# Routing temporaries in PSUM, one reduce for the maxima of k, and a new prologue order

## The chip, the core and the metric

The kernel runs on one core of a Trainium2 chip. Its engines work side by side, each through its own queue in order: PE (TensorE, matrix products and transposes), DVE (VectorE) and ACT (ScalarE) for elementwise work and reductions, POOL (GpSimd) for elementwise work and indirect transfers, SP, whose queue starts most DMAs. SBUF and PSUM are the memories that they read and write; PE writes PSUM alone. The metric is the device time of one execution in microseconds.

## The reference

Three stages follow each other; `k` is normalised over the sequence, `q` over the head.

```python
def _attn_ref(q, k, v):                       # (4, 8, 576, 64)
    q_s = np.exp(q - np.max(q, axis=-1, keepdims=True))
    q_s = q_s / (np.sum(q_s, axis=-1, keepdims=True) + 1e-09)
    k_s = np.exp(k - np.max(k, axis=2, keepdims=True))
    k_s = k_s / (np.sum(k_s, axis=2, keepdims=True) + 1e-09)
    kv = np.einsum('bhsd,bhse->bhde', k_s, v)
    return np.einsum('bhsd,bhde->bhse', q_s, kv)
...
    # _moe_ref: x is (2304, 512), 8 experts 512 -> 1024 -> 512
    noisy_logits = x @ w_gate + np.log1p(np.exp(x @ w_noise)) * noise
    top2 = np.argpartition(-noisy_logits, 2, axis=1)[:, :2]
    ...                                       # softmax over the two
        h = np.maximum(x[mask] @ w1[e], 0.0)
        out[mask] += top2_w[mask, k, None] * (h @ w2[e])
...
    # _moe2_ref: 512 -> 2048 -> 512
    g = P / (Q + 1e-06)                       # P cubic, Q quadratic in h = x @ w_in
    return g @ w_out
```

## The kernel before

Tokens lie on the 128 partitions. The 2304 tokens are 18 tiles of 128: batch `b` gives four tiles of its first 512 tokens (partition p holds tokens 4p to 4p+3, the index `r`), and tiles 8 and 17 hold the last 64 tokens of two batches each (the remainders `kr`, `qr`, `vr` with index `j`). Tiles 0 to 8 are the first half, 9 to 17 the second.

Matrix products in fp32 accuracy for the experts and the last stage take three matmuls (`mm3`, lines 726 to 728): operands are split in a high part, made by ACT, and a low part, made by DVE or POOL. Before that part, called the main loop here, lies a prologue, whose order on every engine is written out by hand: the string `ORDER` names steps (`kmx.1` is step `kmx` with argument 1) and each step issues its instructions in that place, under `tc.manual_schedule`; `REST` follows among the first transposes of the main loop, and `LOADS` orders the loads on SP. A generator step (`rt`, `rl`, `rw`) runs on to its next `yield`. An engine does its instructions in that order and waits for what each needs.

The steps of the prologue:

- k of batch b: `kmx` the maximum over r (DVE, three tensor_tensors over 512 elements), `kmT` transposes it (PE), `kmm` reduces over the partitions' tokens and takes the larger of that and the remainder's `mr` (`krT`, `krm`), `kmB` spreads the maximum (PE, tile `pm`), `ksb` subtracts (DVE, tile `ek`), `kex` (ACT) the exponential, `ksm` (POOL) sums over r, `kz` (PE) over partitions.
- `kv` (PE) is the product of k and v, tile `pk`; `kvn` normalises it into `KV` (name `kvx`, DVE); `kvT`, `kvc` transpose it, `kg` multiplies it with the gate weights and `kgc` copies these 64 columns behind it in `KV`, so that one product with q gives the output of attention and the logits.
- q of batch b: `qmx`, `qsb` (POOL), `qex` (ACT), `qsm` (sum, plus epsilon, reciprocal), `qnm` (POOL, the product). The remainders do the same in `rmx`, `rex`, `rsm`, `rnm`.
- tile T of X: `xT` transposes q (PE), `xc` copies (ACT), `xp` is the product (`px`, two banks of the pool psW), `xo` copies it out (ACT), `xs` stores it as rows of `Xrows` (SP), `xg` sums its logits into `L` (DVE).
- `rt.g`, the routing of half g (`route`): noise, top two of eight, each token's place in its expert's list (`base` is a matmul with counts) and one-hots `oc`, `ocv`, `oh`, three chunks of each, from which `rl` (PE) makes lists; `slots` makes gather and scatter indices; `rw` makes the weights of the two experts. Names in the rows: `u`, `w`, `sp`, `mk`, `ma`, `sc`, `cf`, `ov`.
- expert 0 begins in the prologue on tokens of the first half: `aw` loads its weights, `sa.i` (ACT) and `sv.i` (POOL, line 913; `sv.0.V` on DVE) make high and low parts (`w10l` to `w21l`, two pieces each), `ag` gathers the tokens `xga` (POOL's indirect DMA), `at`, `ac`, `al` (PE, ACT, DVE: `xa`, line 941) transpose and split them; `m1`, `mb` are its first product (`pha`), `mr`, `ml` relu and split, `m2`, `mc` the second (`acca`).

PSUM has eight banks: psT two (`t0`, `t1`), psK two (`k0`, `k1`: `krT`, `kmT`, `pm`, `pk`, `kvT`, `xTa`, `pha` in turn), psW two pairs.

Of the kernel before, what the change touches and what calls it, by code (L numbers as in the profile page):

```python
# [1 line left out]

# [21 lines left out]
E = 8  # L24
# [33 lines left out]
    xg.4 qmx.2 kv.0.2 kv.0.3 qsm.0 rmx.1 qnm.0.1 kz.0 xg.5 rex.1 krm.1 qnm.1.2 kvn.0 kmT.3 qnm.1.3 xT.6 kvT.0
    qmx.3 xc.6 qnm.0.0 xT.7 kvc.0 xp.6 qsb.2 xc.7 xT.1 xo.6 xg.6 xp.7 kmm.3 xc.1 xs.4 xT.0 rsm.1 xo.7 kmB.3 xg.7
    aw.0.0 xc.0 kg.0 ksb.3 qsb.3 qex.2 xT.8 kmT.2 xc.8 aw.0.1 kgc.0 kex.3 kmm.2 xp.1 qnm.0.3 qsm.2 kmB.2 xp.8  # L60
    qnm.0.2 xo.1 xs.5 ksm.3 qex.3 xs.6 xT.2 ksb.2 kv.3.0 aw.1.0 xo.8 xT.3 kv.3.1 xc.2 xc.3 xg.8 sa.0 kv.3.2 xg.1
    qsm.3 xs.8 sa.1 xp.3 aw.1.1 qnm.2.3 kz.3 xo.3 qnm.2.2 kex.2 xg.3 xp.0 sv.0.V kv.3.3 xs.3 xp.2 xs.7 xo.0
    qnm.3.3 xg.0 kvn.3 sa.2 kv.2.0 xs.0 qnm.3.1 xs.1 xg.2 xT.16 rt.0 kv.2.1 ksm.2 xc.16 rt.0 rt.0 xo.2 rt.0
    kv.2.2 sa.3 xs.2 xT.14 kvT.3 xc.14 kv.2.3 kvc.3 kg.3 sa.4 sv.2 kz.2 sa.5 kgc.3 xp.16 kvn.2 sa.6 rt.0 rw.0
    xg.16 xT.12 xo.16 sv.3 rt.0 xp.14 sa.7 xs.16 kvT.2 xo.14 xc.12 xs.14 qnm.3.2 xg.14 xT.11 kvc.2 rt.0 xc.11
    rt.0 xT.15 rw.0 kg.2 xc.15 rt.0 xp.15 qnm.3.0 kgc.2 rt.0 xp.12 xo.15 rt.0 xs.15 xT.13 rt.0 xo.12 rl.0 xc.13
    xs.12 qnm.2.0 xg.15 rl.0 rt.0 xp.13 rt.0 xT.9 xo.13 rt.0 xc.9 xs.13 qnm.2.1 xg.13 rl.0 xg.12 xp.11 rt.0
# [1218 lines left out]
```

## Time and profile before

| what | value |
|---|---|
| median of three runs | 997.84 us (997.36 to 998.83) |
| the profiled execution | 1000.78 us |
| its span, first to last instruction | 998.8 us |
| PE busy | 944.9 us, 95% of the span |
| DVE, ACT, POOL busy | 778.8, 589.4, 283.0 us |
| PE's largest share of the chain that ended last | lines 726 to 728 |
| mean granted clock of PE | .983 of full speed |

The profile cuts the span in 40 slices of 25 us. PE's busy share in tenths reads 2 8 7 7 6 8 9 9 and then 9 in every slice but the last one (8): the first six or seven slices are the prologue. There are two kinds of rows. Timelines give the start in us, the length in us, the engine, the line of the kernel, the operation, what it writes and reads with the shapes, and how many instructions the row joins (x2); in brackets how long the engine was idle before, and whom it waited for. Grouped rows give a sum and the mean of one in ns.

### The profile page before, as it was taken

The numbers are of one execution on the slowest core, as the hardware profiler recorded it, in microseconds if no ns is written. First come the engines' busy times: TensorE is split into PE (matmuls) and PEld (weight loads), VectorE is DVE, ScalarE is ACT, GpSimd is POOL, SyncE is SP. The second block draws the span as 40 slices with busy tenths as digits, with TensorE's granted clock in tenths as the row PEclk, the third lists the DMA queues.
The fourth block names the chain that finished last, engine by engine and source line by source line (L and its number), as shares of the span: only waits on it lengthen the run. The fifth ranks groups of instructions, "written<-read, shape, count | busy, mean of one in ns | idle before, by whom it ended". The sixth has DMA issues, their size and how long they took to land. (4 is left out here: it accounts for less than half of the span.)

```text
span 998.8 us, 15516 instructions
## 1 busy us (share of the span) xinstructions
PE 944.9 (95%) x5296; PEld 845.4 (85%) x5296; DVE 778.8 (78%) x1564; ACT 589.4 (59%) x1188; POOL 283.0 (28%) x279
## 2 busy tenths in 40 slices
PE   2877689999999999999999999999999999999998
PEld 1766678988888888888898999899899999999997
DVE  5887786868677878777871169999989898798785
ACT  3265415545454646455551168787777787787775
POOL 5577422212221212121222133222323222132221
...
GB/s 242 283 214 98 116 14 244 249 161 262 151 243 179 243 205 224 226 200 244 201 173 191 214 320 182 53 95 54 1 74 1 1 43 1 32 1 1 32 1 32
DMA packets 91148, 137.37 MB, mean 138 GB/s; under 512 B 15698, under 2 KB 44374, under 8 KB 91064
## 3 DMA queue, kind: packets, MB, share of 16 engines
...
## 5 line engine op out<-in xcount | busy, mean ns | idle before, releaser
L1141 POOL TENSOR_TENSOR hlr<-vr,hhr 128x384 fp32r<-128x384 f32 x95 | 105.1, 1109 | 287.7 <-ACT hhr L1140 219.4
L726 PE MATMUL phr<-xhr,wih 128*128 128x384 f32 x384 | 129.8, 338 | 0.0
L728 PE MATMUL phr<-xhr,wil 128*128 128x384 f32 x384 | 129.3, 337 | 0.0
L727 PE MATMUL phr<-xlr,wih 128*128 128x384 f32 x384 | 129.0, 336 | 0.0
L791 DVE SCALAR_TENSOR_TENSOR hl<-ph,hh 128x256 fp32r<-128x256 f32 (+4 forms) x120 | 56.6, 471 | 77.8 <-ACT hh L790 75.0
L790 ACT ACTIVATE hh<-ph 128x256 fp32r<-128x256 f32 (+4 forms) x120 | 50.5, 421 | 110.5 <-PE ph L728 104.6
L727 PE MATMUL accr<-wol,hhr 128*128 128x512 f32 x288 | 113.4, 394 | 0.0
L726 PE MATMUL accr<-woh,hhr 128*128 128x512 f32 x288 | 112.7, 391 | 0.0
L728 PE MATMUL accr<-woh,hlr 128*128 128x512 f32 x288 | 109.7, 395 | 0.0
L1129 DVE SCALAR_TENSOR_TENSOR sqr<-sqr,coef,abr 128x384 f32<-128x384 f32 x96 | 64.4, 670 | 35.3 <-ACT sqr L1128 35.3
L756 POOL DMA_INDIRECT xg<-Xrows,gidx x35 | 39.2, 1119 | 160.0 <-PE xT L772 158.4
L1124 ACT ACTIVATE vr<-phr,coef 128x384 f32<-128x384 f32 x96 | 64.1, 668 | 33.1 <-PE phr L728 25.2
L1136 DVE SCALAR_TENSOR_TENSOR sqr<-sqr,qone,abr 128x384 f32<-128x384 f32 x96 | 71.9, 749 | 9.3 <-ACT abr L1135 5.2
L718 POOL DMA_INDIRECT Yrows<-y,sidx x35 | 38.8, 1109 | 135.6 <-ACT y L811 127.2
L1134 ACT ACTIVATE abr<-sqr,qone 128x384 f32<-128x384 f32 x96 | 59.7, 623 | 26.5 <-DVE sqr L1129 26.3
L726 PE MATMUL ph<-xh,w11h 128*128 128x256 f32 (+4 forms) x240 | 75.3, 314 | 0.0
L726 PEld LDWEIGHTS phr<-xhr,wih 128*128 128x128 f32 x384 | 72.2, 188 | 3.4
L727 PEld LDWEIGHTS phr<-xlr,wih 128*128 128x128 f32 x384 | 72.1, 188 | 3.3
L726 PE MATMUL ph<-xh,w10h 128*128 128x256 f32 (+4 forms) x240 | 72.3, 302 | 1.0 <-ACTq L1056 1.0
L727 PE MATMUL ph<-xl,w10h 128*128 128x256 f32 (+4 forms) x240 | 72.7, 303 | 0.1
L728 PE MATMUL ph<-xh,w11l 128*128 128x256 f32 (+4 forms) x240 | 72.6, 302 | 0.0
L727 PE MATMUL ph<-xl,w11h 128*128 128x256 f32 (+4 forms) x240 | 72.4, 302 | 0.0
(293 smaller groups left out, 2652.3 us busy)
## 6 DMA issues: line engine op xcount, KB each, us to landing
...
```

Source lines behind the costliest of these rows:

```text
L718: st = G.indirect_dma_start(out=Y, out_offset=bass.IndirectOffsetOnAxis(ap=idx, axis=0), in_=yt, in_offset=None, bounds_check=2 * NTOK - 1 ...
L726: PE.matmul(o, ah, bh, start=first, stop=False)
L727: PE.matmul(o, ah, bl, start=False, stop=False)
L728: return PE.matmul(o, al, bh, start=False, stop=last).ins
L756: G.indirect_dma_start(out=g[0:self.rows(t)], out_offset=None, in_=X, in_offset=bass.IndirectOffsetOnAxis(ap=self.cols(gidxE, gidx, t), ax ...
L790: a_ = A.activation(hh, ph, AF.Relu)
L791: v_ = V.scalar_tensor_tensor(hl, ph, 0.0, hh.bitcast(F32), op0=ALU.max, op1=ALU.subtract)
L1124: A.activation(v, ph, AF.Identity, scale=coef[:, 3:4], bias=coef[:, 2:3])
L1129: V.scalar_tensor_tensor(sq, sq, coef[:, 5:6], ab, op0=ALU.mult, op1=ALU.add)
L1134: A.activation(r0, sq, AF.Ln, bias=qone)
L1136: V.scalar_tensor_tensor(sq, sq, qone, r0, op0=ALU.add, op1=ALU.mult)
L1141: (V if self.end and f == NF2 - 1 else G).tensor_tensor(gl, v, gh.bitcast(F32), op=ALU.subtract)
```

## The change

- PSUM: psK gets three banks, psW one pair (all `px` tiles take turns on it), and a new pool psR one bank, `route{g}`.
- `route` puts its temporaries in that bank in such a way that each DVE instruction of the chain has an operand there: `u`, `u2`, `sp`, `mk`, `idx`, `po`, `ov2`, `cf`, `ti`, `tr`, later `ma`, `s2`, `oc`, `lvp` in the same columns. `w`, `u3`, `sc`, `ov`, `tj` stay in SBUF; `mk[:, 1]` is copied to SBUF, since both inputs of `ma` would be in PSUM. The counts `rt` come from a reduce. The list values stay in the bank and are copied out once; the weights move from POOL to DVE, with copies of places and experts.
- `kmx` is one tensor_reduce over r, a view with r innermost. The remainder's maxima lie beside those of `kmT`, so that `kmm` is two reduces. `rmx` negates in its reduce.
- epsilon is added by ACT (`qse`, `rse`), `qsm` and `rsm` keep the sum and the reciprocal (`qrc`).
- `kgc` copies by ACT.
- `ORDER` is another one; `LOADS` begins with `kr0`; `mc.6` moves to `REST`.

```diff
-    km1a km1b kr0 qm1 km0 - qr0 - vm1 - vr0 ...
+    kr0 km1a km1b qm1 km0 - qr0 - vm1 - vr0 ...
...
-    xs.9 xg.10 xs.17 rt.1 sv.6 xo.10 rt.1 at.1 at.0 xs.10 ac.1 ac.0 al.1 rt.1 al.0 sv.7 rt.1 m1.0 m1.1 mb.1 sv.4
+    xo.16 xg.16 xc.10 xp.9 rw.0 sv.4 rw.0 rw.0 xo.9 xg.9 xs.9 xp.10 xs.16 sv.5 xg.10 at.1 rt.1 at.0 ac.1 rt.1
+    ac.0 al.1 rt.1 al.0 xo.10 rt.1 m1.0 xs.10 mb.0 m1.1 mr.0 m1.2 mb.1 mb.2 mr.1 mr.2 ml.0 rt.1 rw.1 ml.1 rw.1
...
-    psW = early.enter_context(tc.tile_pool(name="psW", bufs=2, space=PSUM))
-    keyb, qTb = Turn(psK, "k0", "k1"), Turn(psT, "t0", "t1")
+    psW = early.enter_context(tc.tile_pool(name="psW", bufs=1, space=PSUM))
+    keyb, qTb = Turn(psK, "k0", "k1", "k2"), Turn(psT, "t0", "t1")
+    psR = early.enter_context(tc.tile_pool(name="psR", bufs=1, space=PSUM))
...
-        V.tensor_reduce(m, st["kmT", b], axis=AX.X, op=ALU.max)
-        V.tensor_tensor(m, m, st["mr", b // 2][:, :, b % 2], op=ALU.max)
+        mr = st["mr", b // 2][:, b % 2]
+        V.tensor_reduce(mr[:, :, 0], st["kmT", b], axis=AX.X, op=ALU.max)
+        V.tensor_reduce(m, mr, axis=AX.X, op=ALU.max)
...
-    def kgc(b):
-        V.tensor_copy(KV[b][:, :, 2 * HD:], st["pg", b])
+    def kgc(b, eng=A):
+        copy(eng, KV[b][:, :, 2 * HD:], st["pg", b])
...
-        V.tensor_scalar_add(t, t, 1e-9)
-        V.reciprocal(t, t)
+    def plus_eps(t):
+        A.activation(t, t, AF.Identity, bias=eps)
...
-        u = W("u", [P, TP, E], F32, g)[:, 0:n]
-        w = W("w", [P, TP, E], F32, g)[:, 0:n]
-        sp = W("sp", [P, TP, E], F32, g)[:, 0:n]
+        bank = psR.tile([P, 512], F32, tag="r", name=f"route{g}")
+        u, u2, sp = (B_(TP, E) for _ in range(3))
+        mk = B_(2, E, TP)
+        idx, po, ov2, cf = (B_(TP, 2) for _ in range(4))
+        ti, tr = (B_(TP, 2, dt=I32) for _ in range(2))
+        e1s[g] = B_(TP), po, idx
+        at_[0] = 0
+        ma, s2 = (B_(E, TP) for _ in range(2))
+        at_[0] = 0
+        oc = B_(TH * 2, NCOL)
+        lvp = B_(NCOL)
...
-        V.scalar_tensor_tensor(u, w, 1.0, u, op0=ALU.subtract, op1=ALU.subtract)
-        V.scalar_tensor_tensor(u, z, 0.0, u, op0=ALU.max, op1=ALU.subtract)
-        V.tensor_tensor(sp, sp, u, op=ALU.add)
+        V.scalar_tensor_tensor(u2, w, 1.0, u, op0=ALU.subtract, op1=ALU.subtract)
+        V.scalar_tensor_tensor(u3, z, 0.0, u2, op0=ALU.max, op1=ALU.subtract)
+        V.tensor_tensor(sp, sp, u3, op=ALU.add)
...
-        V.tensor_tensor(ma, mk[:, 0], mk[:, 1], op=ALU.add)
+        V.tensor_copy(mk1, mk[:, 1])
+        V.tensor_tensor(ma, mk[:, 0], mk1, op=ALU.add)
...
-        V.tensor_copy(rt, sc[:, :, n - 1])
-        V.tensor_tensor(sc, sc, ma, op=ALU.subtract)
+            V.tensor_reduce(rt, ma, axis=AX.X, op=ALU.add)
+        V.tensor_tensor(s2 if g else sc, sc, ma, op=ALU.subtract)
...
-        V.tensor_scalar(sm, e1, 1.0, 1e-9, op0=ALU.add, op1=ALU.add)
-        V.reciprocal(sm, sm)
-        yield
-        G.tensor_copy(wts[:, ts_, 0], sm)
-        G.tensor_tensor(wts[:, ts_, 1], e1, sm, op=ALU.mult)
+        V.tensor_scalar(e1, e1s[g][0], 1.0, 1e-9, op0=ALU.add, op1=ALU.add)
+        V.reciprocal(wts[:, ts_, 0], e1)
+        V.tensor_tensor(wts[:, ts_, 1], e1s[g][0], wts[:, ts_, 0], op=ALU.mult)
+        V.tensor_copy(pos[:, ts_], e1s[g][1])
+        V.tensor_copy(idf[:, ts_], e1s[g][2])
```

The step `kmx` is in both kernels the same function; `ORDER` of before calls it as `kmx.1.V` (its second branch) and now as `kmx.1` (its first, `km[b].rearrange("p h r d -> p h d r")`).

POOL, around the gather of expert 0's first tokens (`xga`; `eq_...` and `qr_...` are q, `e_0`, `e_1` the weights of the two halves), before:

```order
L404 TENSOR_TENSOR qr_183<-qr_183,qrs_443 128x512
L918 DMA xga_1006<-Xrows,gidxA 128x512
L918 DMA xga_1008<-Xrows,gidxA 128x512
L615 COPY wts<-smw_827 128x9
L616 TENSOR_TENSOR wts<-e_0_826,smw_827 128x9
L913 TENSOR_TENSOR w10l_673<-raw_531,w10h_634 128x1024
L913 TENSOR_TENSOR w21l_1058<-raw_654,w21h_821 128x1024 x2
L913 TENSOR_TENSOR w20l_1136<-raw_615,w20h_800 128x1024 x2
L608 TENSOR_TENSOR e_1_1180<-mv_1085 128x9
```

and now:

```order
L944 TENSOR_TENSOR w10l_691<-raw_523,w10h_669 128x1024
L406 TENSOR_TENSOR eq_518<-eq_518,qs_620 128x512
L406 TENSOR_TENSOR eq_475<-eq_475,qs_609 128x512
L944 TENSOR_TENSOR w11l_809<-raw_601,w11h_708 128x1024
L944 TENSOR_TENSOR w21l_932<-raw_664,w21h_828 128x1024
L406 TENSOR_TENSOR eq_475<-eq_475,qs_609 128x512
L944 TENSOR_TENSOR w21l_932<-raw_664,w21h_828 128x1024
L949 DMA xga_999<-Xrows,gidxA 128x512
L949 DMA xga_1001<-Xrows,gidxA 128x512
L639 TENSOR_TENSOR e_0_1027<-mv_758 128x9
L944 TENSOR_TENSOR w20l_1029<-raw_634,w20h_807 128x1024 x2
L639 TENSOR_TENSOR e_1_1160<-mv_1082 128x9
```

The pieces of `w10l` and `w21l` stood behind the gather and stand ahead of it now; behind it are those of `w20l`.

DVE, at the maxima of batches 2 and 3 (`kmx_382`, `kmx_399` before, `kmx_347`, `kmx_374` now; `kvx` is KV, `mx`, `qs` belong to q), before:

```order
L335 TENSOR_TENSOR kvx_111<-pk_279,rz_332 64x4x64 x2
L293 TENSOR_TENSOR ek_339<-km_144,pm_297 128x8x4x64
L296 TENSOR_TENSOR kr_139<-kr_139,pm_297 64x512
L354 COPY kvx_111<-pg_363 128x4x16
L261 TENSOR_TENSOR kmx_382<-km_164 128x512
L263 TENSOR_TENSOR kmx_382<-kmx_382,km_164 128x512 x2
L261 TENSOR_TENSOR kmx_399<-km_171 128x512
L263 TENSOR_TENSOR kmx_399<-kmx_399,km_171 128x512 x2
L451 TENSOR_REDUCE L<-px_386 128x16
L358 TENSOR_REDUCE mx_417<-qm_174 128x32
L374 TENSOR_REDUCE qs_429<-eq_337 128x32
```

and now:

```order
L340 TENSOR_TENSOR kvx_112<-pk_287,rz_342 64x4x64 x2
L272 TENSOR_REDUCE kmx_347<-km_168 128x512
L272 TENSOR_REDUCE kmx_374<-km_175 128x512
L385 TENSOR_REDUCE qs_390<-eq_325 128x32
L412 RECIPROCAL qrs_327<-qrs_327 128x8
L261 TENSOR_REDUCE mr_425<-krT_354 128x4x2
L402 RECIPROCAL qs_390<-qs_390 128x32
L458 TENSOR_REDUCE L<-px_418 128x16
L369 TENSOR_REDUCE mx_437<-qm_178 128x32
L419 TENSOR_REDUCE mxr_452<-qr_187 128x8
```

The two chains of three instructions are one reduce each, and follow `kvn.1` (`kvx`) directly; `ksb.0` (`ek_339`), which stood between, is earlier now, and the copy from `pg` is gone from this engine.

DVE, at the end of the first half's routing block (`sc`, `rt`), before:

```order
L521 SCALAR_TENSOR_TENSOR sc_764<-seg,ma_762 128x72
L524 CAST rt_766<-sc_764 128x8
L525 TENSOR_TENSOR sc_764<-sc_764,ma_762 128x72
L354 COPY kvx_113<-pg_795 128x4x16
L331 TENSOR_SCALAR rz_816<-pz_804 128x4
L332 RECIPROCAL rz_816<-rz_816 128x4
L335 TENSOR_TENSOR kvx_112<-pk_698,rz_816 64x4x64 x2
L451 TENSOR_REDUCE L<-px_811 128x16
```

now:

```order
L551 SCALAR_TENSOR_TENSOR sc_726<-seg,route_722 128x72
L555 TENSOR_REDUCE rt_783<-route_722 128x8
L556 TENSOR_TENSOR sc_726<-sc_726,route_722 128x72
L336 TENSOR_SCALAR rz_823<-pz_811 128x4
L337 RECIPROCAL rz_823<-rz_823 128x4
L340 TENSOR_TENSOR kvx_113<-pk_682,rz_823 64x4x64 x2
L458 TENSOR_REDUCE L<-px_818 128x16
```

and ACT there now (`w..h` are high parts of expert 0's weights, `qTs` transposed q):

```order
L937 ACTIVATE w11h_708<-raw_601 128x1024
L435 ACTIVATE qTs_792<-qT_746 128x512
L363 ACTIVATE xo_799<-px_700 128x512
L937 ACTIVATE w20h_807<-raw_634 128x1024
L363 ACTIVATE kvx_114<-pg_802 128x4x16
L937 ACTIVATE w20h_807<-raw_634 128x1024
L937 ACTIVATE w21h_828<-raw_664 128x1024
L363 ACTIVATE xo_852<-px_818 128x512
```

The copy from `pg` into `kvx` stood behind the subtraction on DVE and is among the high parts on ACT now.

## Rows read from the trace of the kernel before

**Rows 1.** Stretches (us; busy us per engine, granted clock, DMA share, GB/s).
```profile
127.30:160.00 32.70, 31.21 (x194) 27.65 (x195) 24.43 (x108) 6.63 (x17) 8.54 (x11) 0.92 0.29 97
```

**Rows 2.** Waits of PE, 0 to 160 us (total us, times, longest).
```profile
PE pha L726 <- DVE xa L941: 8.0, 1, 8.0
...
PE px L434 <- DVE kvx L354: 7.4, 2, 5.8
...
PE kmT L275 <- DVE rz L331: 6.2, 1, 6.2
...
PE pm L285 <- DVE m L280: 3.6, 2, 2.5
```

**Rows 3.** Timeline 117 to 128 us (start, length in us; idle before in brackets).
```profile
117.91 8.69 DVE L497 TENSOR_SCALAR w<-u 128x72 f32<-128x72 f32 x1 [0.62 <-ACT u L495]
...
121.90 4.63 POOL L913 TENSOR_TENSOR w20l<-raw,w20h 128x1024 fp32r<-128x1024 f32 x2
...
126.52 1.28 DVE L941 TENSOR_TENSOR xa<-xTa,xa 128x512 fp32r<-128x512 f32 x2
```

**Rows 4.** Timeline, first and second half's routing.
```profile
84.53 0.73 DVE L497 TENSOR_SCALAR w<-u 128x72 f32<-128x72 f32 x1 [0.62 <-ACT u L495]
...
85.29 3.67 DVE L501 SCALAR_TENSOR_TENSOR u<-w,u 128x72 f32<-128x72 f32 x1
...
97.46 1.04 POOL L404 TENSOR_TENSOR qr<-qr,qrs 128x512 f32<-128x512 f32 x1
...
97.51 0.21 DVE L354 COPY kvx<-pg 128x64 f32<-128x64 f32 x1
...
127.72 0.22 DVE L501 SCALAR_TENSOR_TENSOR u<-w,u 128x72 f32<-128x72 f32 x1
...
132.69 0.23 DVE L525 TENSOR_TENSOR sc<-sc,ma 128x72 f32<-128x72 f32 x1
```

**Rows 5.** DVE by line and shape, 0 to 160 us (busy us, mean ns | idle).
```profile
L263 DVE TENSOR_TENSOR kmx<-kmx,km 128x512 f32<-128x512 f32 x8 | 10.3, 1285 | 0.2
...
L358 DVE TENSOR_REDUCE mx<-qm 128x32 f32<-128x2048 f32 x4 | 9.1, 2267 | 0.0
...
L570 DVE TENSOR_TENSOR oh<-rowb,itR 128x768 bf16<-128x768 bf16 x6 | 5.7, 952 | 0.0
...
L567 DVE TENSOR_TENSOR ocv<-oc,vhl 128x288 bf16<-128x288 bf16 x12 | 5.0, 458 | 0.3
...
L261 DVE TENSOR_TENSOR kmx<-km 128x512 f32<-128x512 f32 x4 | 3.8, 957 | 1.4 <-DMA km<-in_k_dram 1.4
...
L540 DVE TENSOR_REDUCE pos<-mk 128x18 f32<-128x144 f32 x2 | 0.8, 421 | 0.1
...
L533 DVE TENSOR_TENSOR sc<-sc,base 128x72 f32<-128x72 f32 x2 | 0.4, 224 | 0.0
```

**Rows 6.** Timeline 99 to 118 us, around the px of the second half.
```profile
99.86 0.21 PE L530 MATMUL base<-rt,tri 128*128 128x8 bf16 x1
...
100.86 1.05 ACT L906 ACTIVATE w21h<-raw 128x1024 fp32r<-128x1024 f32 x1
...
112.35 0.60 ACT L441 ACTIVATE xo<-px 128x512 f32<-128x512 f32 x1 [1.10 <-PE px L434]
...
112.98 0.23 DVE L451 TENSOR_REDUCE L<-px 128x16 f32<-128x64 f32 x1 [0.81 <-ACT xo L441]
...
113.02 4.00 PE L434 MATMUL px<-kvx,qTs 128*128 128x144 f32 x32
```

**Rows 7.** Timeline, k and q part.
```profile
33.60 2.29 DVE L293 TENSOR_TENSOR ek<-km,pm 128x2048 f32<-128x2048 f32 x1
...
55.22 7.20 POOL L366 TENSOR_TENSOR eq<-qm,mx 128x2048 f32<-128x2048 f32 x2
...
59.64 2.80 DVE L280 TENSOR_TENSOR m<-m,mr 128x4 f32<-128x4 f32 x1
```

**Rows 8.** Stretch, columns as in rows 1.
```profile
127.30:129.00 1.70, 1.66 (x6) 1.44 (x7) 1.49 (x6) 0.00 (x0) 0.00 (x0) 0.50 0.00 0
```

More of the change, by code (lines that the diff above doesn't have):

```diff
@@ L1 @@
 from contextlib import ExitStack, contextmanager, nullcontext
+from math import prod
 import concourse.bass as bass
@@ L51 @@
 LOADS = """
-    km1a km1b kr0 qm1 km0 - qr0 - vm1 - vr0 - qm0 - vm0 - km2 - kr1 - km3 - qm2 - vm2 - vr1 qr1 qm3 vm3
+    kr0 km1a km1b qm1 km0 - qr0 - vm1 - vr0 - qm0 - vm0 - km2 - kr1 - km3 - qm2 - vm2 - vr1 qr1 qm3 vm3
 """
 ORDER = """
-    kmx.1.V krT.0 krm.0 kmT.1 kmm.1 qmx.1 kmB.1 ksb.1 qsb.1 rmx.0 kex.1 kmx.0.V qex.1 ksm.1 kmT.0 kv.1.0 kmm.0
-    rex.0 kmB.0 qsm.1 kv.1.1 kv.1.2 rsm.0 qmx.0 kv.1.3 qnm.1.0 kz.1 qnm.1.1 kvn.1 qsb.0 ksb.0 kvT.1 xT.5 kvc.1
-    xT.4 xc.5 xc.4 kg.1 rnm.0 krT.1 kex.0 kgc.1 xp.5 kmx.2.V xp.4 kv.0.0 xo.4 kmx.3.V xo.5 qex.0 kv.0.1 ksm.0
@@ L58 @@
[L58 to L67, printed above, removed]
@@ L73 @@
-    mc.5 m2.7 mc.6
+    krT.0 krm.0 kmx.1 kmT.1 qmx.1 kmm.1 qsb.1 kmx.0 kmB.1 ksb.1 kmT.0 qex.1 kmm.0 kex.1 qsm.1 kmB.0 ksm.1 kv.1.0
+    ksb.0 qse.1 kv.1.1 kv.1.2 qrc.1 kex.0 qmx.0 kv.1.3 qnm.1.2 kz.1 rmx.0 qsb.0 rex.0 kv.0.0 kvn.1 kmx.2 kvT.1
+    krT.1 kv.0.1 rse.0 kvc.1 qnm.1.3 qex.0 xT.6 kmx.3 qnm.1.1 xT.7 kv.0.2 qnm.1.0 xc.6 qsm.0 xc.7 xT.5 ksm.0
+    kg.1 xc.5 xT.4 kgc.1 rsm.0 xp.7 xc.4 krm.1 qse.0 kv.0.3 qrc.0 xo.7 xg.7 qmx.2 xp.4 xo.4 qnm.0.0 kz.0 rmx.1
+    xg.4 rnm.0 rex.1 kvn.0 xp.5 qsb.2 xg.5 kmT.3 kmT.2 qmx.3 kvT.0 rse.1 xT.0 xo.5 xT.8 kvc.0 xp.6 kmm.3 qsb.3
@@ new lines @@
+    xc.0 xg.6 aw.0.0 kmB.3 kmm.2 xo.6 kg.0 xc.8 rsm.1 ksb.3 kmB.2 kgc.0 qex.2 xp.0 qnm.0.3 xs.4 xo.0 xs.6 rnm.1
+    xg.0 xT.3 kex.3 ksb.2 xp.8 xs.7 qnm.0.2 xs.0 qnm.0.1 xs.5 xT.2 qex.3 kv.3.0 aw.0.1 ksm.3 xg.8 qsm.2 kv.3.1
+    xc.2 xo.8 qsm.3 qse.2 xp.2 xc.3 xs.8 kex.2 aw.1.0 xT.1 kv.3.2 qrc.2 xg.2 qnm.2.2 kz.3 qse.3 xo.2 qnm.2.3
+    kv.3.3 qrc.3 aw.1.1 xc.1 qnm.3.0 sa.0 xp.3 kvn.3 qnm.3.1 kv.2.0 xo.3 xg.3 sv.0.V sa.1 kvT.3 xs.3 xp.1 kvc.3
+    xs.2 sa.2 xT.14 qnm.3.2 xg.1 xT.13 rt.0 kv.2.1 ksm.2 xc.14 rt.0 rt.0 xT.15 xc.13 rt.0 kv.2.2 sa.3 xc.15
@@ L139, in fused_kernel, with slots @@
     marks, tiles = {}, {}
-    def slots(pool, lv, n, gi, si, nm):
-        lt = pool.tile([P, n], F32, name=f"lt{nm}")
-        lu = pool.tile([P, n], F32, name=f"lu{nm}")
+    def slots(pool, lv, n, gi, si, nm, tmp=None):
+        lt, lu = tmp or [pool.tile([P, n], F32, name=f"l{x}{nm}") for x in "tu"]
         V.tensor_scalar(lu, lv, float(NTOK), float(-NTOK), op0=ALU.is_gt, op1=ALU.mult)
@@ L351, in kg, with copy, qmx @@
             PE.matmul(pg[:, c], st["kvc", b][:, c, :], wgn[:, c].rearrange("p k e -> p (k e)"), start=True, stop=True)
-    def kgc(b):
-        V.tensor_copy(KV[b][:, :, 2 * HD:], st["pg", b])
-    def qmx(b):
+    def kgc(b, eng=A):
+        copy(eng, KV[b][:, :, 2 * HD:], st["pg", b])
+    def copy(eng, o, i):
+        if eng is A:
+            A.activation(o, i, AF.Copy)
+        else:
+            eng.tensor_copy(o, i)
+    def qmx(b, neg=None):
         mx = st["mx", b] = pw.tile([P, H, R], F32, tag="mx", name=f"mx{b}", bufs=2)
-        V.tensor_reduce(mx, qm[b], axis=AX.X, op=ALU.max)
+        V.tensor_reduce(mx, qm[b], axis=AX.X, op=ALU.max, negate=neg is not None)
     def eq(b):
@@ L490, in route, with B_ @@
         z = L[:, ts_, E:G2E]
-        u = W("u", [P, TP, E], F32, g)[:, 0:n]
-        w = W("w", [P, TP, E], F32, g)[:, 0:n]
-        sp = W("sp", [P, TP, E], F32, g)[:, 0:n]
+        bank = psR.tile([P, 512], F32, tag="r", name=f"route{g}")
+        at_ = [0]
+        def B_(*shape, dt=F32):
+            k = prod(shape)
+            a = bank[:, at_[0]:at_[0] + k]
+            at_[0] += k
+            if dt != F32:
+                a = a.bitcast(dt)
+            ax = "abcd"[:len(shape)]
+            return a.rearrange(f"p ({' '.join(ax)}) -> p {' '.join(ax)}", **dict(zip(ax, shape)))
+        u, u2, sp = (B_(TP, E) for _ in range(3))
[8 more added lines that the diff above has]
+        lvp = B_(NCOL)
+        w = W("w", [P, TP, E], F32, g)
+        u3 = W("u3", [P, TP, E], F32, g)
+        mk1, sc = (W(x, [P, E, TP], F32, g) for x in ("mk1", "sc"))
+        ov = W("ov", [P, TP, 2], F32, g)
+        lt, lu = (W(x, [P, CC], F32, g) for x in ("lt", "lu"))
         A.activation(u, z, AF.Abs)
@@ L981, in fused_kernel @@
     STEPS = {f.__name__: f for f in (krT, krm, kmx, kmT, kmm, kmB, ksb, kex, ksm, kv, kz, kvn, kvT, kvc, kg, kgc,
[L982 removed]
+                                     qmx, qsb, qex, qsm, qse, qxa, qrc, qnm, rmx, rex, rse, rsm, rnm, xT, xc, xp, xo, xs, xg,
                                      aw, sa, sv, ag, eg, at, ac, al, m1, mb, mr, ml, m2, mc, ay)}
```

94 lines of the change are left out of this document (45 added, 49 removed).

## The prediction

> **What bounds the kernel now.** I read the stretches of the span first, then the waits of TensorE (PE) up to 160 us, then the timelines of VectorE (DVE) and GpSimd (POOL) around the longest wait, and last the durations grouped by line and shape. From 127.3 us on PE is busy nearly all the time, 31.21 of 32.70 us in the stretch of [rows 1] and more behind it, so DVE, ACT and POOL can make little shorter there. Before that PE waits often. The change touches only this prologue, so the question is at what time expert 0's first matmul (pha, 127.34 us) starts; what follows takes as long as it did, unless it is said below.
>
> The waits [rows 2] give the candidates: 8.0 us in which pha waits for xa, DVE's low half of the gathered tokens; 7.4 us in which px waits for a copy into kvx on DVE; 6.2 us of kmT behind rz; 3.6 us of pm behind m.
>
> The timelines explain them. In [rows 3] the routing's w, a 128x72 tensor_scalar in SBUF, takes 8.69 us, and both xa come right behind it. POOL subtracts weights up to 121.90 + 4.63 = 126.53, and w ends when POOL does. The same in the first half's routing [rows 4]: STT u takes 3.67 us at 85.29 and .22 at 127.72, where POOL is idle. So DVE work with its operands in SBUF is held while POOL runs a tensor operation. Not all is held: at 97.51 the copy from PSUM takes .21 us although POOL's product runs from 97.46 to 98.50. That is the lever of this change: an instruction with an operand in PSUM gets through.
>
> **The change part by part.** I walk to the start of pha and sum what moves it.
>
> (a) *The stall ahead of pha.* w of the second half now reads a PSUM bank, and of POOL's weight pieces only the two of w20l are left behind the gather; the rest stands ahead of it. In before the last transposes ended 8.0 us ahead of pha, at 119.3; a copy on ACT and one xa (1.28 / 2) then remain, about 1.0 us, so pha could have run at 120.3. Gain 127.3 − 120.3 = 7.0 us. If PSUM operands do not help, the reordered POOL work still leaves less to wait for: bounds 2 and 7.
>
> (b) *The first half's routing block.* From u at 85.29 to the end of the block, where the copy follows at 97.51, are 12.2 us. The same instructions run from 127.72 to 132.69 + .23 = 132.92, 5.2 us, with POOL idle [rows 4]. With w (.73, of which .5 is hold) that is 7.5. The added copy of mk costs about .2 (an SBUF row of that size in rows 4); a reduce in place of a cast nothing. Net −7.3; bounds 0 (all held again) and −7.5. Reading PSUM costs nothing that I can see: adding base from PSUM to 72 elements took .224 us [rows 5], the SBUF row at 127.72 .22. No DVE row of before writes PSUM; I take it at the same price, and allow .1 us either way on each of some 25 instructions, ±2.5.
>
> [...]
>
> (c) *kgc on ACT.* In before the copy of the gate columns sat on DVE behind that block, px waited 5.8 us for it [rows 2], and the base matmul, behind that px on PE, came at 99.86 [rows 6], 2.3 us after the block ended. On ACT the copy stands among hi-splits of 1.05 us. With px out of that chain, I let base follow the block by 1.3: −1.0, bounds 0 and −2.
>
> (d) *The k and q part, up to the routing's start.* Here holds vanish: m of half 3 took 2.80 us at 59.64, while POOL subtracted q for 7.20 us [rows 7]. The four chains of maxima sum to 3.8 + 10.3 = 14.1 us, partly held (L263 at 1285 ns, L261 at 957) [rows 5]. One reduce over 2048 elements takes 2.27 us when contiguous. The new one reads r at a stride of 256 B. The nearest strided row is L540: 144 elements, .421 us. From .23 for 72 (rows 4) and 2.27 for 2048 a contiguous element costs 1.03 ns, so 144 would take .304: .8 ns an element more, 1.65 us over 2048. I take 4.0 us each, nearest to L540; bounds 2.27 and 6. Four make 16, so the reduces by themselves give nothing (+1.9; bounds −5 and +10); they only can no longer be held.
>
> [...]
>
> Walking DVE's new order: kvn.1 ends at 33.6, as before [rows 7], since v lands late anyway. Then kmx.2 and kmx.3 to 41.6, qsm.0, qmx.2, kvn.0 and small ones (8 us), qmx.3 (2.27), kmm.3 (.9): m of half 3 is done at about 53 to 55, where it ended at 62.4 before. That is 8 us earlier; 2 I give back since tiles 0 to 8 share one px pair. The routing starts at 78.3 instead of 84.5: −6.2; bounds 0 (loads or kmx set the pace) and −9. Epsilon on ACT adds a small row and two handovers each time, with the sum queued behind kex's exponentials at worst; that stays inside the bounds.
>
> (e) *One px pair.* With two, four px ran back to back at 4.00 / 4 = 1.0 us a tile [rows 6]. With one, each waits until ACT has copied (.60) and DVE reduced (.23) the last: 1.8 us and the handovers, 2.1 to 2.5 a tile. In before 20.4 us lie between base (99.9) and 120.3. Now nine tiles and 2.3 us of transposes, copy and split for the gathered ones: 9 × 2.3 + 2.3 = 23.0. Cost +2.6; bounds 0 and +8 (xg queued behind one-hot chunks). The gather itself lands earlier than the last tile, if POOL is done with the seven products and splits that now stand ahead of it.
>
> (f) *The clock.* [...] I take −1.0; bounds +1 and −2.6.
>
> Small rows that are added (weights on DVE, copies of positions and of the list, about five of .2 us) stand behind the gather's indices, inside (e)'s bounds. Loads keep their bytes. Sum: −7.0 − 7.3 − 1.0 − 6.2 + 2.6 − 1.0 = −19.9 us. Against the profiled execution (1000.78 us, 2.0 more than its span of 998.8) that is 980.9; it lay 2.9 above the median of 997.84, so for the median **977.9 us**.
>
> **The rivals.**
> (1) *The first 60 us give nothing*: kmx nearer 6 us, or loads, hold (d) at 0, and the px pair costs +6. For it: kmT and pm wait for DVE there [rows 2]. Against it: m of half 3 was late by its hold. −7.0 − 7.3 − 1.0 + 6 = −9.3: 988.5 us.
> (2) *PSUM operands don't free DVE*, since results go to SBUF and back and only one operand is in PSUM. Then (b) is 0, (a) −4 by POOL's order alone, (d) −3, (e) +2.6: 993.4. Against it: the copy at 97.51.
> (3) *Slower, by the px pair*: xo behind a hi-split (1.05 us), xg behind a chunk of one-hots (two L567 and one L570, 1.9 us [rows 5]): 1.0 + 1.05 + .6 + 1.9 + .23 + .3 of handovers = 5.1 us a tile. If that held for nine tiles, (e) would be 9 × 5.1 + 2.3 − 20.4 = +27.8, against 22.5 of gains: +5.3, 1003.1 us. It decides from 4.5 us a tile on. Against it: three chunks and a few splits only stand there.
> (4) *More gain*: kmx at 2.27 (−5 more) and the px pair free (−2.6): −27.5, 970.3.
>
> **How the numbers follow.** The forecast, with a range of its own from 973 to 985, has .60; rival 1 .13, rival 2 .06, rival 3 .07, rival 4 .14. The range of 968 to 990 leaves out rivals 2 and 3 and a piece of 1 and 4. A measurement of this kernel tells .2% (2 us) from no change. Faster .90, within .03, slower .07.
>
> **What would show it.** w of both halves at .2 to .3 us, no row of the routing over .5 while POOL works, pha at 106 to 109 us with its clock at 1.00. kmx at 4 us: below 3 or above 5 the size in (d) was wrong. px of tiles 9 to 17 some 2.3 us apart. The first routing's w at 78 us. If pha is as early as said and the span is not shorter by that much, something moved behind it that I hold unchanged.

## The result, and the profile after

| | before | after |
|---|---|---|
| median | 998.28 us (997.36 to 998.83, 4 runs) | 975.7 us (974.73 to 977.73, 4 runs) |
| ratio to before | | 0.9777, 95% interval 0.9758 to 0.9797 |
| profiled execution, its span | 1000.78, 998.8 us | 974.89, 972.9 us |
| mean granted clock of PE | .983 | .995 |
| PE busy | 944.9 us | 941.4 us |
| start of the first routing (`w`) | 84.53 us | 74.01 us |
| base of the first half | 99.86 us | 81.39 us |
| first `pha` | 127.34 us | 103.72 us |
| from there to the end of the span | 871.5 us | 869.2 us |

The medians lie 22.6 us apart, the two profiled spans 25.9: the profiled execution of before was 2.5 us above its median, that of after .8 below. Of the nine executions of the changed kernel, here and where it is repeated below, six took 974.7 to 976.5 us and three, those with the highest mean granted clock (.998), 977.7 to 979.1. 23.6 us of the 25.9 are won before `pha` starts, 2.3 behind it. In the changed kernel `w` is line 530, the subtractions behind it 534 to 538, `pha` 757, `px` 444, `xg` 458, `kmx` 272.

First what PE waited for up to 150 us (engine, line, what it waited for: us in total, times, longest):

```profile
PE kmT L279 <- DVE kmx L272: 8.2, 2, 5.6
...
PE pm L290 <- DVE m L285: 4.6, 2, 2.8
...
PE px L444 <- DVE L L458: 4.1, 5, 1.9
...
PE pha L757 <- ACT xa L968: 0.9, 1, 0.9
```

Of the waits in [rows 2], `pha` has .9 us left of 8.0 and `px` none for `kvx`; `kmT` no longer waits for `rz`. The waits for `kmx` and for `m` are still there. New are 4.1 us of `px` for `xg`, which come with the one px pair.

The timeline of DVE and of POOL over the first routing (start, length in us; idle before in brackets), which answers [rows 4]:

```profile
73.61 2.64 POOL L267 TENSOR_TENSOR ks<-ks,ek 128x512 f32<-128x512 f32 x2
...
74.01 0.23 DVE L530 TENSOR_SCALAR w<-route 128x72 f32<-128x72 f32 x1 [0.74 <-ACT route L528]
...
74.64 0.24 DVE L534 SCALAR_TENSOR_TENSOR route<-w,route 128x72 f32<-128x72 f32 x1 [0.40 <-ACT route L532]
...
77.57 2.34 POOL L944 TENSOR_TENSOR w11l<-raw,w11h 128x1024 fp32r<-128x1024 f32 x1
...
78.27 0.32 DVE L547 TENSOR_TENSOR route<-route,it 128x144 f32<-128x144 f32 x1
...
79.50 0.22 DVE L556 TENSOR_TENSOR sc<-sc,route 128x72 f32<-128x72 f32 x1
```

POOL works from 71.2 to 92.2 us with pauses under .1 us, and no row of the routing takes more than its price: `w` .23 instead of .73, the first subtraction .24 instead of 3.67. From 74.01 to 79.72 the block takes 5.71 us; before, 12.98 up to the copy behind it.

The stretch that PE now fills, and the one around the first `pha` (columns as in [rows 1]):

```profile
60.00:80.00 20.00, 20.00 (x152) 17.91 (x150) 14.43 (x55) 16.32 (x27) 19.42 (x16) 1.00 0.68 216
...
106.00:112.00 6.00, 5.61 (x41) 4.90 (x40) 5.61 (x43) 1.33 (x4) 0.21 (x1) 1.00 0.02 4
```

Between 60 and 80 us PE is busy all the time. In the last stretch the granted clock is 1.00, where [rows 8] had .50.

### The profile page after: what moved, and what is told of

Read it like the earlier page. It is cut to its first block, busy times and chain, and to the rows that moved or that the text cites. A ratio compares the mean times of both kernels' runs of the same rounds, so it can differ in the third digit from the quotient of the medians.

```text
span 972.9 us, 15490 instructions
## 1 busy us (share of the span) xinstructions
PE 941.4 (97%) x5296; PEld 841.8 (87%) x5296; DVE 757.7 (78%) x1552; ACT 591.0 (61%) x1198; POOL 281.7 (29%) x276
```

## The experiments

Each kernel is compared with the kernel before on the same chip, so ratios are set against each other. The main question is whether DVE instructions with their operands in SBUF are held while POOL works, so that PSUM makes the gain, or whether the order alone makes it. Each expectation names its own two theories.

### The routing temporaries in SBUF, the new order kept

```diff
-        bank = psR.tile([P, 512], F32, tag="r", name=f"route{g}")
+        bank = pw.tile([P, 512], F32, tag="r", name=f"route{g}", bufs=1)
```

> The kernel after the change, with one edit: the bank of routing temporaries is a tile in SBUF instead of PSUM; the order is the new one. Theory 1 (DVE work with all its operands in SBUF is held while POOL works): POOL was busy from 71.2 to 92.2 us in the changed kernel, so the first routing block (74.0 to 79.7 there) is held again by some 5 to 8 us, single rows of it take 1 to 3 us, base comes at 87 to 89 instead of 81.4, the chunks of one-hots are held too; the whole is 5 to 9 us slower than the changed kernel (981 to 985). Theory 2 (the new order makes the gain, the memory of the operands matters little): block within 1 us of 5.7, time within 1 us of 975.7.

Measured 993.71 us, ratio 0.9945 (0.9928 to 0.9961): by the ratios 1.7%, some 17 us, slower than the changed kernel, through one line. Theory 1 holds, but I had its size too small. Timeline of DVE and POOL at the first routing:

```profile
72.32 2.63 POOL L267 TENSOR_TENSOR ks<-ks,ek 128x512 f32<-128x512 f32 x2
...
73.68 1.37 DVE L534 SCALAR_TENSOR_TENSOR route<-w,route 128x72 f32<-128x72 f32 x1
...
75.03 1.27 POOL L311 TENSOR_TENSOR ks<-ks,kr 64x512 f32<-64x512 f32 x1
...
75.08 5.95 DVE L535 SCALAR_TENSOR_TENSOR u<-L,route 128x72 f32<-128x72 f32 x1
...
76.27 2.35 POOL L944 TENSOR_TENSOR w11l<-raw,w11h 128x1024 fp32r<-128x1024 f32 x1
...
78.58 2.35 POOL L944 TENSOR_TENSOR w10l<-raw,w10h 128x1024 fp32r<-128x1024 f32 x1
...
82.06 5.56 DVE L537 TENSOR_TENSOR route<-route,nz 128x72 f32<-128x72 f32 x1
...
92.01 0.23 DVE L556 TENSOR_TENSOR sc<-sc,route 128x72 f32<-128x72 f32 x1
```

The block takes 72.79 to 92.24, 19.5 us instead of 5.7. The subtraction at 73.68 ends when POOL's pair does (72.32 + 2.63). The next row over 72 elements starts right then, as POOL's next does, and takes 5.95 us: it ends .1 us behind the third POOL instruction from there; the next but one takes 5.56. So here a held row isn't let through at each end of a POOL instruction. That is why I had expected too little: I counted one POOL instruction for a hold (1 to 3 us), though the 8.69 us of [rows 3] had been longer than that already.

### The order of before, with POOL's pieces ahead of the gather

```diff
-    rnm.1 xo.11 ... sv.1 ... sv.6 ... sv.7
+    rnm.1 sv.1 sv.6 sv.7 xo.11 ...
```

> The kernel before, with one edit of its order: the three POOL pieces that stood behind the gather ahead of w20l (w10l's second and both of w21l) stand ahead of the gather, behind rnm.1. Theory 1: w of the second routing is held only until w20l ends, so it falls from 8.69 us to 1 to 3, but now POOL works from 98.5 to 105.5, where the one-hot chunks of the first half (all in SBUF) run, and holds them by 3 to 6 us; net gain 1 to 5 us (993 to 997). Theory 2: the stall of 8 us goes and nothing comes for it, gain 6 to 8 us (990 to 992).

Measured 995.71 us, ratio 0.9962 (0.9949 to 0.9974), 3.9 us faster. Timeline of DVE:

```profile
99.63 2.51 DVE L539 TENSOR_TENSOR mk<-mk,sc 128x144 f32<-128x144 f32 x1
...
102.62 1.76 DVE L546 CAST ti<-pos 128x18 int32<-128x18 f32 x1
...
120.14 1.82 DVE L497 TENSOR_SCALAR w<-u 128x72 f32<-128x72 f32 x1 [0.62 <-ACT u L495]
...
121.95 1.29 DVE L941 TENSOR_TENSOR xa<-xTa,xa 128x512 fp32r<-128x512 f32 x2
```

`w` falls from 8.69 to 1.82 us (6.9), and POOL's earlier work holds the routing's product at 99.63 (2.51 instead of .30) and the cast behind it (1.76 instead of .18) instead. `pha` starts at 122.79, 4.5 us earlier. With operands in SBUF the POOL work can be moved, but part of its price moves with it: 3.8 of the 6.9 us in these two rows. I had expected the one-hot chunks to be hit; it was the rows ahead of them.

### The changed kernel, POOL's pieces behind the gather

```diff
-    ... sv.6 rt.0 rt.0 rl.0 ... sv.7 xo.12 ... rw.0 sv.4 rw.0
+    ... rw.0 sv.6 sv.7 sv.4 rw.0
```

> The kernel after the change, with the two POOL pieces of w21l moved from ahead of the gather to behind it, ahead of w20l, so that POOL works from 97.6 to 107 us, over w and the first rows of the second routing. Theory 1: with operands in PSUM nothing is held: w .23, the rows after it .24 to .32, first pha at 103 to 104.5, time within 1.5 us of 975.7. Theory 2 (the changed kernel lost its stall because POOL was done in time, not through PSUM): w takes 3 to 5 us, pha comes 3 to 5 us later, time 979 to 981.

Measured 975.14 us, ratio 0.9767 (0.9750 to 0.9784), the changed kernel's time. POOL works from 96.5 to 105.85 us over the second routing:

```profile
96.52 4.68 POOL L944 TENSOR_TENSOR w21l<-raw,w21h 128x1024 fp32r<-128x1024 f32 x2
...
101.14 4.71 POOL L944 TENSOR_TENSOR w20l<-raw,w20h 128x1024 fp32r<-128x1024 f32 x2
...
101.65 0.23 DVE L530 TENSOR_SCALAR w<-route 128x72 f32<-128x72 f32 x1 [0.55 <-ACT route L528]
...
102.15 1.29 DVE L972 TENSOR_TENSOR xa<-xTa,xa 128x512 fp32r<-128x512 f32 x2 [0.27 <-ACT xa L968]
...
103.36 0.23 DVE L534 SCALAR_TENSOR_TENSOR route<-w,route 128x72 f32<-128x72 f32 x1
...
104.43 0.24 DVE L538 TENSOR_TENSOR route<-route,L 128x72 f32<-128x72 f32 x1
```

`w` .23, both `xa` .65, the subtractions .23 and .24. In the changed kernel POOL was done at 102.3, ahead of `w` at 102.71, so its own trace could not tell whether the stall had gone through PSUM or through POOL's order. This run does: POOL beside it costs nothing.

### Both: routing in SBUF and POOL's pieces late

> Both edits together on the changed kernel: routing temporaries in SBUF, and the two POOL pieces of w21l behind the gather. Theory 1: the first block is held a little less than with the early pieces (POOL is free sooner), and w of the second routing is held until POOL is done, 4 to 9 us, with xa and pha behind it: 9 to 15 us slower than the changed kernel (985 to 991), and PE's clock falls in that hole. Theory 2: within 3 us of the run with the late pieces alone.

Measured 994.96 us, ratio 0.9957 (0.9940 to 0.9973): some 18 us slower than the changed kernel, more than either theory said.

```profile
108.02 4.64 POOL L944 TENSOR_TENSOR w21l<-raw,w21h 128x1024 fp32r<-128x1024 f32 x2
...
109.14 8.15 DVE L643 TENSOR_SCALAR e<-route 128x9 f32<-128x9 f32 x1 [0.36 <-ACT route L641]
...
112.62 4.62 POOL L944 TENSOR_TENSOR w20l<-raw,w20h 128x1024 fp32r<-128x1024 f32 x2
...
121.32 0.20 DVE L530 TENSOR_SCALAR w<-route 128x72 f32<-128x72 f32 x1 [0.69 <-ACT route L528]
```

The hold hit another row than expected: the first instruction of the weights (`e`, 9 elements) took 8.15 us, through both pairs of POOL's subtractions. `xg` stood behind it and the px pair behind `xg`, so PE waited 8.0 us there. `w` came later and was free.

### The new order alone

The edits put back: routing in SBUF, three tensor_tensors for each maximum of k, a tensor_tensor for the larger maximum, epsilon and the gate columns' copy on DVE.

```diff
-        V.tensor_reduce(m, mr, axis=AX.X, op=ALU.max)
+        V.tensor_tensor(m, mr[:, :, 0], mr[:, :, 1], op=ALU.max)
-        A.activation(t, t, AF.Identity, bias=eps)
+        V.tensor_scalar_add(t, t, 1e-9)
-    ... kmx.1 ... kgc.1 ...
+    ... kmx.1.V ... kgc.1.V ...
```

> The kernel after the change, with the instructions of before put back into the new order and the new PSUM pools: routing temporaries in SBUF, the maxima of k in three tensor_tensors each, the larger of two maxima by a tensor_tensor, epsilon and the gate columns' copy on DVE. So it shows what the new order (with one px pair and a third bank for k) does alone. Theory 1 (the gain is DVE getting through beside POOL, and the order can be so dense only because of that): as slow as before or slower, 996 to 1008, since with SBUF routing alone it was 993.7 and the other edits put back more held rows. Theory 2 (order is a gain of its own): 985 to 992.

Measured 1005.96 us, ratio 1.0068 (1.0044 to 1.0093): slower than before. Theory 2 falls. Its first and last row of the first routing:

```profile
84.32 0.95 DVE L530 TENSOR_SCALAR w<-route 128x72 f32<-128x72 f32 x1 [0.81 <-ACT route L528]
...
103.65 0.23 DVE L556 TENSOR_TENSOR sc<-sc,route 128x72 f32<-128x72 f32 x1
```

The routing starts as late as in the kernel before (84.53), and the block then takes 19.6 us. The changed kernel with two banks for k's tiles instead of three gave no time: its steps wait for each other in a circle and it can't run through. So this order needs the third bank, and what that bank is worth in time isn't measured.

### The same with the routing in PSUM

> The new order with the instructions of before put back everywhere (maxima of k in three tensor_tensors, tensor_tensor for the larger maximum, epsilon and the gate columns' copy on DVE), but the routing temporaries in PSUM. Order alone was 1006.0 us, order with all edits but PSUM 993.7, all edits 975.7 to 976.5. If the two groups of edits add up, it is 1006 - 18 = 988 us (985 to 991), the routing block takes 5.7 us again, and what is left of the gap sits in front of the block: epsilon and m held beside POOL, kgc behind them. If PSUM routing alone is the lever and the others only matter with it held, 976 to 980.

Measured 985.32 us, ratio 0.9859 (0.9842 to 0.9875). By the ratios PSUM routing gives 2.1% (21 us) on the bare order and 1.7% (17 us) beside the other edits; the others give .8% with it and 1.2% without. The two groups nearly add up. Timeline of DVE:

```profile
56.70 3.06 DVE L285 TENSOR_TENSOR m<-mr 128x4 f32<-128x4 f32 x1
...
84.04 0.23 DVE L530 TENSOR_SCALAR w<-route 128x72 f32<-128x72 f32 x1 [0.74 <-ACT route L528]
...
84.67 0.24 DVE L534 SCALAR_TENSOR_TENSOR route<-w,route 128x72 f32<-128x72 f32 x1 [0.40 <-ACT route L532]
...
89.54 0.22 DVE L556 TENSOR_TENSOR sc<-sc,route 128x72 f32<-128x72 f32 x1
```

The same maximum `m` in the changed kernel, as a reduce:

```profile
53.67 0.16 DVE L285 TENSOR_REDUCE m<-mr 128x4 f32<-128x8 f32 x1
```

The routing starts at 84.04 and takes 5.7 us. Its start is that of before; so the new order by itself doesn't move it, and the 10 us by which the changed kernel starts it earlier come only with the small edits ahead of it (here `m`, 3.06 us instead of .16). What these edits would give in the order of before was not run.

### The gate columns' copy on DVE

```diff
-    ... kg.1 xc.5 xT.4 kgc.1 ...
+    ... kg.1 xc.5 xT.4 kgc.1.V ...
```

> The kernel after the change with the gate columns' copies back on DVE, at the same places of the order. The prediction gave this part 1.0 us, since in the kernel before the copy sat behind the held routing block. Theory 1 (the copy was late only because the block was held): the copy of batch 3 comes at about 79.8 us, right when its matmul is done, and the time is within 1.5 us of the changed kernel. Theory 2 (ACT is the better place in any case): DVE's queue delays px of the first tiles behind the maxima of k (33.6 to 41 us) and the time is 2 to 4 us longer.

Measured 980.32 us, ratio 0.9816 (0.9794 to 0.9838), 3.9 us slower than the changed kernel beside it (976.47; ratio 0.9778, 0.9763 to 0.9792, so the intervals just miss each other); by the profiled spans, 976.1 and 972.9 us, it is 3.2. Theory 2 holds. Its timeline of DVE and its waits of PE:

```profile
33.29 7.51 DVE L272 TENSOR_REDUCE kmx<-km 128x512 f32<-128x2048 f32 x2
...
43.03 0.22 DVE L365 COPY kvx<-pg 128x64 f32<-128x64 f32 x1
```

```profile
PE px L444 <- DVE kvx L365: 6.1, 3, 3.2
```

The copy of batch 1 comes only at 43.03, behind both maxima (33.29 to 40.80) and a sum of q (to 42.99), and `px` waits 3.2 us for it; for that of batch 0, at 58.26, it waits 2.4. The place that the prediction named (batch 3, behind the routing block) costs nothing once the block is free; another does.

### Epsilon on DVE

```diff
-        A.activation(t, t, AF.Identity, bias=eps)
+        V.tensor_scalar_add(t, t, 1e-9)
```

> The kernel after the change with epsilon added by DVE (tensor_scalar in SBUF) instead of ACT, at the same places of the order. Theory 1 (SBUF rows are held beside POOL): the tensor_scalars take 1 to 4 us each where POOL runs (six of them, after 22 us), 4 to 10 us in all on DVE, and the time is 1 to 6 us longer than the changed kernel. Theory 2 (that edit is worth nothing): within 1 us.

Measured 978.06 us, ratio 0.9784 (0.9769 to 0.9800), against 0.9778 (0.9763 to 0.9792) of the changed kernel beside it: the intervals overlap, so its worth in the time is not settled. Theory 1 finds little in its rows of DVE: the first sum is held, .85 us, the second takes .31, the others .16 to .17, not 4 to 10 us together. Still its routing starts at 78.30 us, 4.3 later than in the changed kernel's profile. That comes from PE. Two of its rows, the same product of k and v, of this kernel and of the changed one:

```profile
29.37 2.07 PE L317 MATMUL pk<-vm,ek 128*128 128x128 f32 x8
```

```profile
28.20 1.16 PE L317 MATMUL pk<-vm,ek 128*128 128x128 f32 x8
```

In this profile PE makes eight of these in 2.07 us at 26.64, 29.37 and 32.09 us, with 8 to 11 matmuls in each 2 us from 26 to 38 us; the changed kernel makes eight in 1.16 us from 28.20 us on, and its repeated profile has 17 matmuls in the 2 us from 28. The step from 2.07 to 1.16 us, a factor of 1.8, is that of `px` between a granted .50 (2.29 us for eight at 97.78 in the kernel before) and 1.00 (1.25). Yet the profile has the granted clock at 1.00 in both from 20 to 40 us, so in these first 40 us it doesn't tell PE's rate; what sets the moment isn't shown. From `kmx` of batch 2 to the routing's start this run takes 40.3 us (38.02 to 78.30), the changed kernel 40.4 (33.59 to 74.01): epsilon costs nothing there, and nothing shows that it has a part in PE's later moment.

### The maxima of k

Three tensor_tensors each (`kmx.1.V` and so on), all else new:

> The kernel after the change with the maxima of k in three tensor_tensors each again, all else new. The strided reduce measured 3.62 to 3.77 us each. Theory 1: kmx.1 takes 2.1 us (POOL idle), but kmx.0, kmx.2 and kmx.3 run beside POOL and take 3 to 7 us each, 14 us or more in all against 14.8, so that the time is 0 to 5 us longer than 975.7 (975 to 981). Theory 2 (the reduce gives nothing): the same within 1 us or up to 2 us faster.

Measured 976.02 us, ratio 0.9773 (0.9743 to 0.9804), as the changed kernel. In its profiled execution the routing starts at 75.56 us, 1.6 later, but `pha` at 103.69, as there, since the first `px` behind base takes 1.20 us and in the changed kernel's, where the granted clock falls to .57, 2.12 (point (e) of the account below). And the reduce over four neighbours instead of the four tokens, which reads SBUF in order:

```diff
-            V.tensor_reduce(t, km[b].rearrange("p h r d -> p h d r"), axis=AX.X, op=ALU.max)
+            V.tensor_reduce(t, km[b].rearrange("p h r (d x) -> p h (r d) x", x=R), axis=AX.X, op=ALU.max)
```

> The kernel after the change with the reduce of the maxima over four neighbouring elements of the head instead of the four tokens r, so that it reads SBUF in order. (It then subtracts, per column, a maximum of other elements of the same head; the softmax over tokens doesn't depend on that constant.) If the stride is what makes 3.62 of 2.27 us, each takes 2.27 to 2.3 us, all four are 5.4 us shorter. Theory 1 (this part of DVE's queue sets when the second stage of k comes): 3 to 5 us faster than 975.7 (971 to 973). Theory 2 (loads set the pace in the first 50 us): within 1.5 us of 975.7.

Measured 973.51 us, ratio 0.9748 (0.9718 to 0.9778). The maxima on DVE: of the changed kernel grouped by line and shape (busy us, mean ns), then the timelines of the three operations and of the reduce in order:

```profile
L272 DVE TENSOR_REDUCE kmx<-km 128x512 f32<-128x2048 f32 x4 | 14.8, 3731 | 1.1 <-DMA km<-in_k_dram 1.1
```

```profile
8.50 0.69 DVE L265 TENSOR_TENSOR kmx<-km 128x512 f32<-128x512 f32 x1 [1.24 <-DMA km<-in_k_dram]
...
37.73 1.53 DVE L265 TENSOR_TENSOR kmx<-km 128x512 f32<-128x512 f32 x1
...
39.29 3.35 DVE L267 TENSOR_TENSOR kmx<-kmx,km 128x512 f32<-128x512 f32 x2
```

```profile
8.27 2.29 DVE L272 TENSOR_REDUCE kmx<-km 128x512 f32<-128x2048 f32 x1 [1.20 <-DMA km<-in_k_dram]
...
35.04 2.29 DVE L272 TENSOR_REDUCE kmx<-km 128x512 f32<-128x2048 f32 x1 [1.57 <-DMA km<-in_k_dram]
```

The strided reduce takes 3.73 us, the one in order 2.29. Three operations take 2.1 us at 8.50 to 10.65, where POOL is idle in the changed kernel's profile, and 4.9 at 37.73 to 42.64 (there POOL works from 36.50 to 41.88), 15.8 in all against 14.8: in the time the strided reduce gains nothing over them that shows, as the prediction said. In order the four are 5.7 us shorter, but at 35.04 the reduce waits for its load. Its profiled execution has `pha` 2.1 us earlier (101.65), of which 1.6 are again the stretch behind base, whose first `px` takes 1.21 us. Whether the order of reading is worth 2 us or nothing is asked again:

### Both edits that measured no worse, and the changed kernel again

> The changed kernel with both edits that measured no worse: the reduce of the maxima over four neighbouring elements (a constant per column, which the softmax over tokens doesn't depend on) and the two POOL pieces of w21l behind the gather. From 2.3 us (973.5 against 976 in one batch) and about 0: 972 to 975, 1 to 3 us faster than the changed kernel beside it, pha at 100 to 102 us.

> The changed kernel itself, unchanged, beside the three others on the same chip: 974 to 977 us, a ratio to the kernel before of .976 to .979.

Measured 975.71 us, ratio 0.9767 (0.9748 to 0.9786), against 976.47 us, ratio 0.9778 (0.9763 to 0.9792): no difference that can be measured, and not the 1 to 3 us expected. They start `pha` at 102.5 and 102.6 us. So no version here beats the changed kernel beyond doubt.

## Why the prediction was right, point by point

- **What bounds it.** Only the start of `pha` counts: yes. It came 23.6 us earlier and the span is 25.9 shorter; the other runs have 868.7 to 870.5 us from `pha` to the end, before had 871.5.
- **(b) the routing block, −7.3.** Measured 12.98 − 5.71 = −7.3, and a subtraction with an operand or the result in PSUM takes .23 to .24 us where .23 was read in SBUF (`w` .23 and, with SBUF alone and unheld, .20). The term is right to a tenth.
- **(a) the stall ahead of `pha`, −7.0.** `pha` waits .95 us for ACT and .4 for `xa`, as it should without a hold. The run with POOL late shows that PSUM is enough for it, whatever POOL's order; that order alone, in the kernel before, takes 6.9 us off `w` and gives 3.8 back in other rows. The trace doesn't part (a) from (e): from base to `pha` before took 27.5 us and the changed kernel 22.3, −5.1 for both together, said −4.4.
- **(c) `kgc`, −1.0.** Base follows the block by 1.67 us (81.39 − 79.72), before by 2.3: −.6. But putting the copy back cost 3 to 4 us, at the copies of batches 1 and 0 behind the maxima and `ek`. The step looked only where before had waited.
- **(d) up to the routing, −6.2.** Here the sum is off most: −10.5 (74.01 us, said 78.3). The walk was good up to `m` of half 3 (53.8 us, said 53 to 55). Wrong was the step "2 I give back since tiles 0 to 8 share one px pair": between 60 and 80 us PE is busy 20.00 of 20.00, so the px pair cost nothing there, and the stretch from the end of `ek` of half 3 to the routing's start, 18.6 us before (65.97 to 84.53), which I had let grow, shrank to 16.6 (57.42 to 74.01). The runs with edits put back show what the gain is made of: the new order alone moves the routing's start by .2 us, with the small edits it is 10 us earlier. Without them `m` takes 3.06 us instead of .16; put back one at a time, the gate columns' copy starts the routing at 76.34 and the three tensor_tensors at 75.56, against 74.01 and 72.84 in the changed kernel's two profiles, and epsilon shows no part.
- **The maxima.** 4.0 us taken, 3.62 to 3.77 measured; nothing gained over three operations in the time, as said.
- **(e) one px pair, +2.6.** From base to `pha` 22.3 us instead of the 20.4 unheld of before: +1.9. That this came near is luck. The sum counted nine tiles behind base, but one of the nine px, at 80.33 us, stands ahead of it: 8 × 2.3 + 2.3 = 20.7. That is what three runs take: 20.7 us each with three tensor_tensors, with the reduce in order and with epsilon on DVE. Their first `px` behind base takes 1.20, 1.21 and 1.21 us, and in the last of them the granted clock is 1.00 from 80 to 100 us. In the changed kernel the granted clock is .57 from 82 to 86 us, after those 20 us in which PE was never idle, and the first px there takes 2.12 us. So of the 1.9 us 1.6 are the clock, for which the prediction has no term at this place, and .3 are left for the px pair. (The 20.4 of before hold some .9 us of low clock themselves, .57 from 99.86 to 102; at full clock the pair costs about 1.2, an estimate.) Why the clock falls in some runs and not in others isn't shown. The later px are 2.2 us apart, said 2.1 to 2.5. First the stretch (columns as in [rows 1]), then PE's rows:

```profile
80.00:100.00 20.00, 17.50 (x133) 15.44 (x132) 12.55 (x46) 11.05 (x20) 16.89 (x12) 0.91 0.33 99
```

```profile
83.43 2.12 PE L444 MATMUL px<-kvx,qTs 128*128 128x144 f32 x8
...
93.98 1.25 PE L444 MATMUL px<-kvx,qTs 128*128 128x144 f32 x8 [0.22 <-DVE L L458]
...
96.22 1.25 PE L444 MATMUL px<-kvx,qTs 128*128 128x144 f32 x8 [0.56 <-DVE L L458]
...
98.41 1.25 PE L444 MATMUL px<-kvx,qTs 128*128 128x144 f32 x8 [0.51 <-DVE L L458]
...
103.72 0.39 PE L757 MATMUL pha<-xa,w10h 128*128 128x256 f32 x1 [0.95 <-ACT xa L968]
```

- **(f) the clock, −1.0.** From `pha` to the end −2.3, within its bounds; in the repeated changed kernel it was −1.2 (870.3 us). No run shows the −1.0 by itself. What the runs show in its place: the granted clock is 1.00 from `pha` on, where [rows 1] had .92 over 32.70 us (8% of them are 2.6 us, an estimate), and base of the second half waits only .4 us for the routing.
- **The sum.** −19.9 said, −25.9 between the profiled spans, −22.6 between the medians: of the 6.0 us between the first two, 4.3 are (d), 1.3 (f) and .7 (e), and (c) gave .4 less than said. In the median the miss is smaller, 2.2 us, since the two profiled executions lay 2.5 above and .8 below theirs; that part of the nearness is luck.
- **The rivals.** (2), PSUM operands don't free DVE, is refuted by the runs in SBUF. (3), the px pair as the bound, needed 4.5 us a tile; 2.2 to 3.1 were measured. (1), nothing in the first 60 us, is refuted by the routing's start. (4), more gain, is half right: the px pair cost about 1 us, but the maxima took 3.7 us each and not 2.27, and the rest of the surplus came from (d).

Held in these runs were tensor_tensors (5.56 us) and scalar_tensor_tensors (5.95) with two SBUF inputs, and tensor_scalars (8.69) and casts (1.76) from SBUF to SBUF with one. Not held in any row of the prologue's timelines were a reduce, a reciprocal or a row with one side in PSUM (the copy at 97.51 in [rows 4], .21 us). In the kernel before, the reduce and the reciprocal with POOL idle (12.39, 27.40), then beside it:

```profile
12.39 2.28 DVE L358 TENSOR_REDUCE mx<-qm 128x32 f32<-128x2048 f32 x1
...
27.40 0.35 DVE L376 RECIPROCAL qs<-qs 128x32 f32<-128x32 f32 x1
...
54.22 2.29 DVE L358 TENSOR_REDUCE mx<-qm 128x32 f32<-128x2048 f32 x1
...
55.22 7.20 POOL L366 TENSOR_TENSOR eq<-qm,mx 128x2048 f32<-128x2048 f32 x2
...
69.33 2.63 POOL L263 TENSOR_TENSOR ks<-ks,ek 128x512 f32<-128x512 f32 x2
...
70.67 0.35 DVE L376 RECIPROCAL qs<-qs 128x32 f32<-128x32 f32 x1
```

By what mechanism POOL's work holds a row isn't shown.
